# Cosine attention and a hard-swish MLP on one core: the written-out order of pairs 0 to 17 is replaced by another

## The chip, the cores and the metric

The kernel runs on one NeuronCore of one Trainium2 chip. The core has five engines that run their own instruction queues in order and wait for one another through semaphores: TensorE (PE; its weight loads are listed as PEld), VectorE (DVE), ScalarE (ACT), GpSimd (POOL) and SyncE (SP), which here only issues DMAs. The metric is the device time of one launch in microseconds (us). The kernel before takes 404.92 us, the median of three runs (403.64, 404.92 and 406.51).

## The reference: what is computed

```python
q_n = q / (np.linalg.norm(q, axis=-1, keepdims=True) + 1e-06)
k_n = k / (np.linalg.norm(k, axis=-1, keepdims=True) + 1e-06)
scores = np.matmul(q_n, k_n.transpose(0, 1, 3, 2)) / tau
attn = softmax(scores)                       # over the last axis
x = np.matmul(attn, v)                       # then heads side by side: (3584, 768)
h = x @ w_in                                 # (3584, 2048)
g = h * np.clip(h + 3.0, 0.0, 6.0) / 6.0
out = g @ w_out                              # (3584, 768), float32
```

q, k and v have 8 batches, 12 heads, 448 rows and 64 columns. The excerpt is shortened: the softmax of the reference is written out with its maximum and its sum.

## The kernel before, in words

**Tiling.** Two heads make a pair, so there are 8 x 6 = 48 pairs, and six pairs make a batch. Loads, squares and norms work on items: item j is q or k for two pairs, 128 partitions by 896 float32 (448 KB). For the first items the two pairs' halves (448 columns each) can also be handled apart. For a pair the kernel squares, sums over the head dimension, takes the norm, scales the rows, transposes them on TensorE, copies the transposes out of PSUM, multiplies K by Q (scores), takes the exponential on ScalarE, multiplies by V (values), divides by the sum, and transposes the result back into `xT`, the MLP's input. When the six pairs of a batch are in `xT`, the MLP of that batch can run: 16 units of six matmuls with `w_in` (each followed by a relu on ScalarE and a product on VectorE), and later the products with `w_out`.

**What sets the order.** Pairs 18 to 47 are written by a loop that repeats. Pairs 0 to 17 are written out as a list, `PLAN` (line 21), of tokens, which `run` (line 973) turns into instructions one after another. Each engine executes its own instructions in exactly that order. An instruction waits only for what it reads and for the buffer that it writes, so a token far down the list can start at once when its engine is free, and a token whose input is late holds up everything behind it on its engine. The loads (`LQ`, `LV`) are issued by SyncE in list order too.

**The tokens.** The number behind the name is the item j or the pair i. A letter `a`, `v` or `p` names the engine: ScalarE, VectorE or GpSimd.

- `LQ.j` loads item j (line 197), `LV.d` loads V for two pairs with four DMAs (line 212), `W` issues one load of weights from GpSimd's queue (line 923).
- `SQ.j.e.c.n` squares n column groups of item j from group c on engine e (lines 227 and 229). `RE.j` sums the squares on VectorE (line 241); a further number means one half.
- `NO.d` makes 1/norm of items 2d and 2d+1: four small ScalarE operations (lines 269, 270, 275, 276), or with `v` two on ScalarE and two on VectorE (lines 272, 273).
- `NM.j.e` multiplies item j by 1/norm (line 286); a further number means one half. On VectorE, this and `SQ` read two operands from SBUF.
- `TR.j` transposes item j on TensorE (line 332). `CQ.i`, `CK.i`, `CS.i` copy Q and K of pair i out of PSUM (line 354 on VectorE, 352 on ScalarE).
- `SC.i.g` is group g of the scores (lines 432 and 435), `EX.i.g` its exponential (line 453); up to pair 5 the exponential of groups 0 to 2 is one instruction of 128x896, from pair 6 on it is two of 128x448.
- `VC.i.e` casts V of pair i (line 305; on VectorE line 303), `VA.i.g` multiplies by V (line 475), `FI.i` divides by the sums (lines 495, 496).
- `BK.i` transposes back (line 509), `CX.i` copies into `xT` (line 354 or 352); later pairs use DMA transposes (`XD`, `XB`, `XP`).
- `U` is the next matmul unit of the MLP (line 580 for `w_in`, line 627 for `w_out`), `UA` and `UV` its work on ScalarE and VectorE (lines 589 and 595). The 36 units of the plan belong to batches 0 and 1.
- `WS` and `GL` are sums and copies of weights and of `gT` on VectorE.
- `DP.n` and `D.n` are n matmuls on zeros, whose results nobody reads (lines 935 and 930). `OPEN` (`open_ring`) frees the PSUM of the first six pairs and makes six banks, which scores, transposes and units use in turn from then on.

The two banks (`SC`) of the first six pairs are used in turn: scores of a group wait until the exponential of the group before last has read its bank.

Of the kernel before, what the change touches and what calls it, by code (L numbers as in the profile page):

```python
# [1110 lines left out]
```

## Time and profile before

The profiled execution's span, from its first to its last instruction, is 404.4 us; the median of the three unprofiled runs is 404.92 us.

| engine | busy, us | share of the span | instructions |
|---|---|---|---|
| TensorE matmul | 393.7 | 97% | 3689 |
| TensorE weight load | 234.5 | 58% | 3689 |
| VectorE | 288.7 | 71% | 512 |
| ScalarE | 276.7 | 68% | 604 |
| GpSimd | 236.7 | 59% | 232 |

The granted TensorE clock is 1.000 over the span. The 16 DMA engines move 63.75 MB. Matmuls are pipelined: a group of six matmuls with `w_in` takes 1.14 us in the chain of work although one of them is listed with 352 ns, so a busy TensorE in these rows is not yet one that works at its full rate.

How to read the rows that follow: a row of the timeline gives the start and the length in us, the engine, the line of the kernel, the operation, what it writes and reads with shapes, how many instructions are merged in the row, and in brackets how long the engine had been idle and what released it. A row of stretches gives the busy time of each engine within the stretch. A row of a group gives the count, the busy time and the mean length in ns.

### The profile page before, as it was taken

The numbers are of one execution on the slowest core, as the hardware profiler recorded it, in microseconds if no ns is written. First come the engines' busy times: TensorE is split into PE (matmuls) and PEld (weight loads), VectorE is DVE, ScalarE is ACT, GpSimd is POOL, SyncE is SP. The second block draws the span as 40 slices with busy tenths as digits, with TensorE's granted clock in tenths as the row PEclk, the third lists the DMA queues.
The fourth block names the chain that finished last, engine by engine and source line by source line (L and its number), as shares of the span: only waits on it lengthen the run. The fifth ranks groups of instructions, "written<-read, shape, count | busy, mean of one in ns | idle before, by whom it ended". The sixth has DMA issues, their size and how long they took to land.

```text
span 404.4 us, 9618 instructions
## 1 busy us (share of the span) xinstructions
PE 393.7 (97%) x3689; PEld 234.5 (58%) x3689; DVE 288.7 (71%) x512; ACT 276.7 (68%) x604; POOL 236.7 (59%) x232
## 2 busy tenths in 40 slices
PE   7798999999999999999999999999999999999996
PEld 5566656555665555655555556555565556555564
DVE  5898787878498777777857887587656666655663
ACT  4899989887377687687768768768758755225230
POOL 4799945862744997588486875876664600510070
PEclk9999999999999999999999999999999999999999
DMA  8899999999877748786779659986863523140134
GB/s 285 247 235 243 221 221 213 170 219 202 181 168 179 167 111 209 185 222 129 169 200 194 140 149 163 180 190 136 193 147 76 112 45 63 36 88 20 25 74 99
DMA packets 93166, 63.75 MB, mean 158 GB/s; under 512 B 56128, under 2 KB 93120, under 8 KB 93120
## 3 DMA queue, kind: packets, MB, share of 16 engines
q1 hardware_dynamic: 87408, 56.45, 61.1%
q0 software_dynamic: 5312, 6.29, 9.5%
q8 instruction: 29, 0.48, 0.6%
q10 hardware_dynamic: 400, 0.39, 0.3%
q14 instruction: 17, 0.14, 0.1%
HBM read 45.61 MB, written 11.01 MB: 140 GB/s over the span
## 4 chain that ended last, share of the span: by engine, by line
PE 88%; ACT 4%; DVE 3%; DMA 3%; SPq 1%; issue 0%; DVEq 0%; ACTq 0%
PE M L580 23%; PE M L753 16%; PE PV L475 11%; PE Y L580 6%; PE Z L580 6%; PE M L435 6%; PE Z L753 5%; PE Y L753 4%; PE M L833 3%; PE M L627 3%; ACT at L453 3%; DMA big<-in_q_dram 3%; PE Y L435 1%; PE Z L435 1%; PE Y L833 1%; PE Y L627 1%
## 5 line engine op out<-in xcount | busy, mean ns | idle before, releaser
L453 ACT ACTIVATE at<-M 128x448 bf16<-128x448 f32 x194 | 96.8, 564 | 23.2 <-PE M L435 20.7
L580 PEld LDWEIGHTS <-w_in_sb 128*128 128x128 bf16 x768 | 72.3, 98 | 63.1 <-issue 2.5
L580 PE MATMUL M<-xT,w_in_sb 128*128 128x448 bf16 x504 | 107.4, 352 | 0.1
L286 POOL TENSOR_TENSOR nrm<-big,r 128x896 bf16<-128x896 f32 (+1 forms) x47 | 78.1, 1665 | 14.8 <-issue 4.6
L229 POOL TENSOR_TENSOR big<-big 128x896 f32<-128x896 f32 (+5 forms) x45 | 68.1, 1519 | 14.8 <-DMA big<-in_k_dram 8.2
L589 ACT ACTIVATE u<-M,bias 128x448 bf16<-128x448 f32 x84 | 54.9, 655 | 26.3 <-PE M L580 26.0
L475 PEld LDWEIGHTS <-at 128*128 128x128 bf16 (+1 forms) x1536 | 54.1, 97 | 19.9 <-issue 12.1
L595 DVE SCALAR_TENSOR_TENSOR gT<-u,M 128x448 bf16<-128x448 bf16 x73 | 44.6, 617 | 29.2 <-ACT u L589 28.4
L475 PE MATMUL PV<-vx,at 128*128 128x65 bf16 (+1 forms) x1536 | 62.7, 194 | 0.0
L241 DVE TENSOR_REDUCE n<-big 128x14 f32<-128x896 f32 (+1 forms) x50 | 51.5, 1037 | 0.3 <-ACT big L227 0.2
L392 POOL COPY km<-tT 64x128 bf16<-64x128 bf16 x34 | 14.4, 424 | 61.9 <-PE M L435 25.9
L782 POOL TENSOR_TENSOR big<-big 128x384 f32<-128x384 f32 x11 | 11.8, 1077 | 54.6 <-ACT big L801 54.5
L753 PEld LDWEIGHTS <-gT 128*128 128x128 bf16 x288 | 27.8, 98 | 20.0 <-DVE gT L731 0.6
L753 PE MATMUL M<-w_out_sb,gT 128*128 128x384 bf16 x192 | 35.0, 326 | 0.1
L496 DVE TENSOR_TENSOR on<-PV,rc 128x512 bf16<-128x512 f32 x48 | 33.2, 691 | 1.7
L435 PE MATMUL M<-tT,kz 64*128 64x448 bf16 (+1 forms) x171 | 30.9, 351 | 0.5 <-ACT at L453 0.5
L453 ACT ACTIVATE at<-Y 128x448 bf16<-128x448 f32 x50 | 28.2, 564 | 4.3 <-PE Z L435 4.3
L753 PEld LDWEIGHTS <-gs 128*128 128x128 bf16 x224 | 21.5, 98 | 14.7 <-DVE gs L731 0.3
L453 ACT ACTIVATE at<-Z 128x448 bf16<-128x448 f32 x50 | 28.2, 565 | 2.6 <-PE M L435 2.6
L305 POOL CAST vx<-big 128x512 bf16<-128x512 f32 x39 | 28.2, 728 | 3.1 <-DMA big<-in_v_dram 3.0
L580 PE MATMUL Z<-xT,w_in_sb 128*128 128x448 bf16 x132 | 28.6, 353 | 0.0
L580 PE MATMUL Y<-xT,w_in_sb 128*128 128x448 bf16 x132 | 28.6, 352 | 0.0
(128 smaller groups left out, 574.7 us busy)
## 6 DMA issues: line engine op xcount, KB each, us to landing
big<-in_k_dram SPq DMA_DIRECT2D x24, 448.0 KB, 5.1
big<-in_q_dram SPq DMA_DIRECT2D x24, 448.0 KB, 4.5
out_dram<-o SPq DMA_DIRECT2D x107, 96.0 KB, 2.2
big<-in_v_dram SPq DMA_DIRECT2D x48, 128.0 KB, 4.7
big<-in_v_dram SPq DMA_DIRECT2D x48, 96.0 KB, 4.4
w_in_sb<-in_moe_w_in_dram POOLq DMA_DIRECT2D x8, 384.0 KB, 10.4
w_out_sb<-in_moe_w_out_dram POOLq DMA_DIRECT2D x4, 768.0 KB, 10.8
tT<-nrm SPq DMA_TRANSPOSE x34, 2.8
```

What stands on the lines that cost most here:

```text
L229: engines[e].tensor_tensor(out=o, in0=i, in1=i, op=ALU.mult)
L241: nc.vector.tensor_reduce(out=n2_and_r[0][:, d % 2, j % 2, c], in_=sq[:, :, :, :].rearrange("p g c d -> p (g c) d")[:, c, :], axis=AX.X, o ...
L286: engines[e].tensor_tensor(out=nrm[:, :, g, :].rearrange("p c g d -> p g c d"), in0=raw_of[j][:, g, :, :], in1=n2_and_r[4][:, d % 2, j % 2, :]
L305: (engines[e].copy if e == "a" else engines[e].tensor_copy)(out=o, in_=f)
L435: nc.tensor.matmul(o, ks, qt[rows], start=True, stop=True)
L453: nc.scalar.activation(out=o, in_=x, func=AF.Exp, scale=inv_tau)
L475: nc.tensor.matmul(pv_out(j, h), at[rows, n, q_cols(i // HP, j)], vt[rows, 3 + h if name == "M" else 5 * h + int(name[1]), :], start=(name ...
L496: nc.vector.tensor_tensor(out=on[:, :, :, :].rearrange("p j h d -> p h j d"), in0=pv4[:, :, :, 0:D], in1=rc[:, :, :].to_broadcast([128, 2, ...
L580: nc.tensor.matmul(ps[:, 0:S], w_in_sb[:, cc, fc * 128 : (fc + 1) * 128], x[:, cc, 0:S], start=(cc == 0), stop=(cc == CC - 1),)
L589: nc.scalar.activation(out=u[:, :], in_=ps[:, 0:S], func=AF.Relu, bias=half_bias, scale=1.0 / 6.0)
L595: nc.vector.scalar_tensor_tensor(out=g[:, fc, c0 : c0 + S], in0=u[:, :], scalar=1.0, in1=ps[:, 0:S], op0=ALU.min, op1=ALU.mult,)
L753: nc.tensor.matmul(m, lhs[:, c, :], rhs[:, c, c0 : c0 + width], start=(base is None and c == 0), stop=(c == KC - 1), skip_group_check=True,)
```

## The change: another list for pairs 0 to 17

All lines of `PLAN` are replaced; no function, no tile and nothing from pair 18 on is changed. The new list holds the same attention and MLP work. These things differ:

- The order. Item 0 is loaded before item 1. 41 matmuls on zeros stand together ahead of the first transpose; in all there are 90 of 248 columns, where the list before had 87, and two of 512 columns that are gone.
- The engine of some operations. Of the squares, counted in items of 896 columns, GpSimd has 9.9 instead of 14.8, ScalarE 8.8 instead of 5.6, VectorE 4.3 instead of 2.6. Of the scaling (`NM`), GpSimd has 15.5 items instead of 17.5 and VectorE 5.5 instead of 3.5. Of the casts of V, GpSimd keeps 11, ScalarE has 7 instead of 2 and VectorE 2 instead of 7. Four norms instead of two use VectorE for their second half. Of the copies into `xT`, VectorE has 9 instead of 7 and ScalarE 1 instead of 3; ScalarE has two copies of Q instead of one.

The diff, cut to the part up to the first unit (`U`) and a few later lines:

```diff
--- before.py
+++ after.py
 PLAN = [
-    "DP.1 LQ.1 DP.2 DP.1 DP.1 DP.1 DP.1 DP.1 SQ.1.a.0.4 SQ.1.a.7.4 DP.1 SQ.1.v.4.3 DP.1 SQ.1.p.11.3 LQ.0 DP.2 DP.3",
-    "LQ.3 DP.1 LQ.2 SQ.0.p.6.2 RE.1.0 RE.1.1 LQ.5 DP.2 SQ.0.a.0.6 SQ.0.p.8.6 DP.1 RE.0.0 RE.0.1 DP.1 NO.0.1 DP.1 DP.1",
-    "NM.1.v.1 DP.1 SQ.3.a.0.7 DP.1 LQ.4 DP.2 D.2 DP.1 DP.2 NM.1.v.0 LV.0 DP.1 DP.2 NO.0.0.v DP.4 SQ.2.a.0.7 TR.1.Y",
-    "CK.1.a DP.1 DP.1 DP.1 DP.2 RE.3 DP.1 RE.2 NM.0.p.1 CK.0.a SQ.5.a.4.3 DP.2 DP.1 DP.4 DP.1 LQ.8 NM.0.p.0",
-    "SQ.4.v.4.3 SQ.5.a.0.4 NO.1 DP.1 DP.2 SQ.4.p.0.4 LV.1 TR.0.Z DP.3 DP.1 DP.1 NM.3.p LQ.7 NM.2.p.0 CQ.0.v SC.0.0.0",
-    "RE.5 LQ.6 DP.1 DP.1 EX.0.0 SC.0.1.1 DP.1 RE.4 NM.2.v.1 EX.0.1 DP.1 DP.1 NO.2 NM.4.p DP.1 LQ.10 VC.0.v DP.1 DP.2",
-    "LQ.9 DP.1 SC.0.2.0 SC.0.3.1 TR.3.Y CQ.1.v VC.1.v LV.2 CK.2.v DP.2 DP.2 DP.1 DP.1 VC.2.v EX.0.2 SQ.7.p.0.7 LQ.11",
-    "W EX.0.3 TR.2.Z CQ.2.v SC.1.0.0 EX.1.0 SC.1.1.1 CQ.3.v DP.1 SC.1.2.0 TR.4.Z VC.3.v EX.1.1 EX.1.2 SC.1.3.1 VA.0.0",
-    "CQ.4.v EX.1.3 DP.1 CQ.5.v LV.4 DP.2 LV.3 SQ.6.a.0.7 NM.5.v.1 W DP.1 DP.1 RE.7 SC.2.0.0 RE.6 VA.0.1 NM.5.p.0",
-    "SC.2.1.1 VA.0.2 VA.0.3 SQ.8.p.0.7 EX.2.0 EX.2.1 DP.3 SQ.9.p.0.7 DP.1 SC.2.2.0 FI.0 CK.3.v TR.5.Z SC.2.3.1 EX.2.2",
-    "CK.4.v NO.3.v NM.6.p RE.8 VA.1.0 VA.1.1 SC.3.0.0 VA.1.2 VA.1.3 EX.2.3 SC.3.1.1 FI.1 EX.3.0 SC.3.2.0 EX.3.1",
-    "EX.3.2 SC.3.3.1 EX.3.3 VA.2.0 SQ.10.p.0.7 RE.9 SQ.11.p.0.7 W NM.7.p.0 VC.4.p CK.5.v DP.1 VA.2.1 VA.2.2 VA.2.3",
-    "FI.2 VC.5.p LQ.13 NO.4 SC.4.0.0 TR.6.Y SC.4.1.1 EX.4.0 CQ.6.v CQ.7.v VA.3.0 VA.3.1 RE.10 VA.3.2 NM.8.p SC.4.2.0",
-    "BK.2.Z EX.4.1 EX.4.2 VC.6.p VA.3.3 NM.9.p W W VC.7.p LQ.12 LV.5 SC.4.3.1 SC.5.0.0 CX.2.v NM.7.v.1 FI.3 EX.4.3",
-    "BK.0.Y CX.0.v SC.5.1.1 EX.5.0 EX.5.1 SC.5.2.0 BK.3.Y DP.1 RE.11 TR.7.Z CX.3.v VA.4.0 VA.4.1 SQ.13.p.0.7 CK.6.v",
-    "SC.5.3.1 EX.5.2 BK.1.Y NO.5 NM.10.p EX.5.3 OPEN VA.4.2 CK.7.v SQ.12.p.0.7 SC.6.0 DP.1 CS.7.v VA.4.3 EX.6.0",
-    "CX.1.v CS.6.v SC.6.1 SC.6.2 TR.8 SC.6.3 EX.6.1 W W LQ.15 FI.4 VA.5.0 BK.4.Y VA.5.1 VA.5.2 CQ.8.v CQ.9.v EX.6.2",
-    "VC.8.p CX.4.v SC.7.0 VA.5.3 VC.9.p FI.5 TR.9 SC.7.1 EX.6.3 EX.7.0 SC.7.2 SC.7.3 CK.8.v CS.9.v CK.9.v VA.6.0",
-    "VA.6.1 CS.8.v VA.6.2 VA.6.3 BK.5 CX.5.v EX.7.1 SC.8.0 LQ.17 EX.7.2 EX.7.3 U EX.8.0 NM.11.p SC.8.1 SC.8.2 FI.6",
...
-    "UA CX.8.v U VA.12.3 SC.13.0 UV SC.13.1 UA FI.12 UV EX.13.0 U XD.14 VC.13.a SQ.19.a.0.4 SQ.19.p.4.3 GL.0 SC.13.2",
-    "SQ.18.v.0.7 U EX.13.1 VA.13.0 SC.13.3 CS.14.v XD.15 U VA.13.1 UA RE.19 LQ.21 UA UV U CK.14.a UV W EX.13.2",
...
-    "U FI.16 CK.18.v UA U WS.y4.0 SC.17.3 EX.17.3 CS.18.v CK.19.v UV XB.16 VA.17.0 NM.20.v",
+    "LQ.0 SQ.0.a.8.6 SQ.0.p.6.2 RE.0.1 SQ.0.a.0.6 RE.0.0 LQ.1 SQ.1.a.0.4 SQ.1.a.11.3 SQ.1.p.4.3 RE.1.0 LQ.2 LQ.3",
+    "SQ.1.p.7.4 RE.1.1 NO.0.0 NM.0.v.0 NO.0.1 NM.1.v.1 SQ.2.a.0.7 NM.1.v.0 NM.0.p.1 DP.4 DP.4 DP.4 DP.4 DP.4 DP.4",
+    "DP.4 DP.4 DP.4 DP.4 DP.1 TR.0.Z CQ.1.v CQ.0.a DP.2 TR.1.Y CK.0.v DP.4 DP.1 SC.0.0.0 RE.2 SQ.3.a.0.7 RE.3",
+    "SC.0.1.1 CK.1.v LQ.4 LQ.5 EX.0.0 EX.0.1 LV.0 SQ.5.v.0.4 LQ.7 W NO.1.v DP.4 DP.4 SC.0.2.0 DP.3 SC.0.3.1 LQ.6",
+    "SQ.5.v.4.3 EX.0.2 EX.0.3 DP.4 DP.2 SC.1.0.0 DP.1 SC.1.1.1 EX.1.0 NM.2.v.1 DP.4 SC.1.2.0 NM.2.v.0 LV.1 LQ.8",
+    "SQ.4.a.4.3 EX.1.1 TR.2.Z RE.5 SQ.4.p.0.4 RE.4 EX.1.2 NM.3.p DP.3 SC.1.3.1 EX.1.3 TR.3.Y VC.0.p LQ.9 VA.0.0",
+    "VA.0.1 CQ.2.v CK.2.v VA.0.2 VC.1.p VA.0.3 CK.3.v NO.2.v FI.0 SQ.7.a.0.7 RE.7 SC.2.0.0 LV.2 CQ.3.v NM.4.p VC.2.p",
+    "SC.2.1.1 EX.2.0 DP.4 DP.3 SC.2.2.0 SQ.6.a.0.7 NM.5.p.0 RE.6 VA.1.0 VA.1.1 VA.1.2 VA.1.3 FI.1 TR.4.Z CQ.5.v",
+    "CQ.4.v EX.2.1 SC.2.3.1 EX.2.2 EX.2.3 VC.3.p LV.4 BK.0.Y LV.3 LQ.11 CX.0.v DP.1 SC.3.0.0 DP.1 SC.3.1.1 NO.3.v",
+    "NM.5.p.1 W VA.2.0 W VA.2.1 VA.2.2 VA.2.3 EX.3.0 EX.3.1 NM.7.p.0 SC.3.2.0 EX.3.2 LQ.10 NM.6.p NM.7.p.1 SQ.8.p.0.7",
+    "SQ.9.v.0.7 BK.1.Y LQ.13 TR.5.Z CK.4.v SC.3.3.1 EX.3.3 DP.2 SC.4.0.0 DP.1 SC.4.1.1 FI.2 DP.1 VA.3.0 EX.4.0 EX.4.1",
+    "VA.3.1 VA.3.2 VA.3.3 CX.1.v CK.5.v LQ.14 RE.9 BK.2.Z SC.4.2.0 SC.4.3.1 CX.2.v TR.6.Y FI.3 VC.4.a CQ.6.v TR.7.Z",
+    "VC.5.p EX.4.2 SC.5.0.0 LQ.12 EX.4.3 CQ.7.v CK.6.v VA.4.0 CS.6.v SC.5.1.1 VA.4.1 VA.4.2 VA.4.3 W EX.5.0 SC.5.2.0",
+    "RE.8 BK.3.Y EX.5.1 EX.5.2 W FI.4 CX.3.v SC.5.3.1 CS.7.v NO.4 EX.5.3 OPEN CK.7.v DP.3 SC.6.0 BK.4.Y VA.5.0 VA.5.1",
+    "VA.5.2 CX.4.v DP.1 VA.5.3 EX.6.0 SC.6.1 SC.6.2 EX.6.1 NM.8.v FI.5 VC.6.p TR.8 CQ.8.v SC.6.3 W VA.6.0 VA.6.1",
+    "EX.6.2 EX.6.3 CQ.9.v BK.5 SC.7.0 CX.5.v EX.7.0 NM.9.v SQ.11.p.0.7 RE.11 VA.6.2 SC.7.1 SC.7.2 VA.6.3 FI.6 EX.7.1",
+    "EX.7.2 U SQ.10.p.0.7 VC.8.p TR.9 VC.7.a CK.8.a SC.7.3 CS.9.v EX.7.3 RE.10 CK.9.v U VA.7.0 VA.7.1 VA.7.2",
+    "SQ.13.p.0.7 UA UA VC.9.p CS.8.v UV U NO.5 SC.8.0 SC.8.1 UV UA EX.8.0 NM.11.p UV EX.8.1 U UA UV VA.7.3 FI.7",
...
+    "RE.16 LQ.21 EX.13.3 U SQ.18.a.0.7 U UV UV GL.0 VC.14.a CK.15.v LQ.20 FI.12 VA.13.0 UA SQ.19.p.0.4 UA UA U U U",
+    "VA.13.1 VA.13.2 RE.19 RE.18 SQ.21.a.0.7 SQ.20.a.0.7 UV UV UA VC.15.p UA UV UV UA NN.8 U UV UV UA UV SC.14.0",
+    "EX.14.0 W W SC.14.1 EX.14.1 LV.9 LV.8 U UA VA.13.3 FI.13 UV U U UA UA CS.14.v SC.14.2 NM.16.p EX.14.2 SC.14.3",
+    "XD.16 NM.19.p RE.20 VC.16.a U VA.14.0 VA.14.1 NM.17.v XD.17 RE.21 XP.12 UV UV EX.14.3 UA SC.15.0 SC.15.1 SC.15.2",
+    "EX.15.0 SQ.22.v.4.3 EX.15.1 EX.15.2 VA.14.2 VA.14.3 FI.14 VC.18.a LQ.23 U SC.15.3 CK.17.a CK.16.v NM.18.p",
+    "EX.15.3 CS.16.v WS.6 XD.18 U UA UV NO.10.v VA.15.0 VA.15.1 SC.16.0 SC.16.1 EX.16.0 SC.16.2 WS.7.1 EX.16.1",
+    "VA.15.2 VC.17.a VA.15.3 FI.15 XP.14 WS.7.0 XD.19 U UV SC.16.3 VA.16.0 VC.19.a CK.18.v VA.16.1 EX.16.2 WS.1 LV.11",
...
+    "SC.17.3 CK.19.a UV CS.18.v VA.17.0 SQ.22.v.0.4 XB.16 EX.17.3",
 ]
```

27 rows, old and new, of the table PLAN are left out of this document.

## The prediction

> **What bounds the kernel now.** I read the page first, then the stretches of the span, then the timeline of the opening, then ScalarE's groups.
>
> ```profile
> span 404.4 us, 9618 instructions
> PE 393.7 (97%) x3689; PEld 234.5 (58%) x3689; DVE 288.7 (71%) x512; ACT 276.7 (68%) x604; POOL 236.7 (59%) x232
> ```
> ```profile
> 4.28:14.90 10.62, 9.02 (x70) 6.84 (x68) 7.47 (x14) 7.02 (x20) 4.96 (x6) 1.00 0.95 299
> 14.90:44.00 29.10, 26.71 (x396) 17.96 (x396) 26.27 (x62) 27.97 (x53) 28.53 (x25) 1.00 1.12 247
> 44.00:117.00 73.00, 72.90 (x715) 42.21 (x715) 55.45 (x100) 56.66 (x126) 41.17 (x38) 1.00 1.01 199
> 117.00:341.00 224.00, 223.87 (x2155) 131.69 (x2152) 163.24 (x265) 165.67 (x373) 145.62 (x136) 1.00 0.69 154
> ```
> The stretches give, after the length, the busy us of PE, PEld, DVE, ACT and POOL. The last one quoted is the loop of pairs 18 and up: PE is busy 223.87 of 224.00 us, so what happens there can't be hastened by an order of pairs 0 to 17; it can only begin earlier or later. The same is nearly true from 44 us on. Between 14.90 and 44.00 it is another matter: ACT (27.97), POOL (28.53) and DVE (26.27 of 29.10) are all nearly full, and PE fills its time with attention and zeros. So the kernel's time is a fixed amount of PE work behind the first MLP unit, plus the time at which that unit can start. The question is when it starts after the change, and whether PE stays fed from there to pair 18.
>
> ```profile
> 2.47 5.55 PE L935 MATMUL PV<-xT 128*128 128x248 bf16 x26 [2.47 <-DVE vx L988]
> 4.28 0.72 ACT L227 ACTIVATE big<-big 128x256 f32<-128x256 f32 x2 [2.26 <-DMA big<-in_k_dram]
> 5.49 0.52 ACT L227 ACTIVATE big<-big 128x384 f32<-128x384 f32 x1 [0.49 <-DMA big<-in_q_dram]
> 6.11 1.26 DVE L241 TENSOR_REDUCE n<-big 128x7 f32<-128x448 f32 x2 [0.22 <-ACT big L227]
> 7.29 1.15 DVE L286 TENSOR_TENSOR nrm<-big,r 128x448 bf16<-128x448 f32 x2
> 8.40 1.22 PE L935 MATMUL PV<-xT 128*128 128x248 bf16 x10
> 9.46 0.55 PE L332 MATMUL Y<-ident,nrm 128*128 128x128 bf16 x7
> 9.81 0.94 ACT L227 ACTIVATE big<-big 128x896 f32<-128x896 f32 x1
> 10.47 1.83 POOL L286 TENSOR_TENSOR nrm<-big,r 128x448 bf16<-128x448 f32 x2 [3.75 <-DVE r L273]
> 12.36 0.56 PE L332 MATMUL Z<-ident,nrm 128*128 128x128 bf16 x7 [0.55 <-POOL nrm L286]
> 13.59 0.56 DVE L229 TENSOR_TENSOR big<-big 128x384 f32<-128x384 f32 x1 [1.27 <-DMA big<-in_q_dram]
> 14.06 0.38 DVE L354 COPY tT<-Z 128x448 bf16<-128x448 bf16 x1
> 14.50 0.36 PE L435 MATMUL SC<-tT,kz 64*128 64x448 bf16 x2 [1.05 <-DVE tT L354]
> 14.90 1.73 ACT L453 ACTIVATE at<-SC 128x896 bf16<-128x896 f32 x2 [0.99 <-PE SC L435]
> ```
> The reader is to see a late first score. K of pairs 0 and 1 is transposed at 9.46, but Q is scaled on POOL only at 10.47, behind a norm whose end waits for other work, and transposed at 12.36. Its copy out of PSUM then stands on DVE behind a square whose load comes at 13.59. So scores start at 14.50 and exponentials at 14.90.
>
> **The change part by part.**
>
> *The opening.* Item 0 takes item 1's place in the queue of loads, so its squares start at 4.28 and item 1's at 5.49. DVE still makes four half reduces and ends them at about 7.3, as now (6.11 + 1.26). The first norm runs beside them, so the first half `NM` on DVE starts at about 7.3. The second norm's four ACT operations take about 1.1 us to 8.4; two more halves on DVE at 1.15 for two end at 9.6, and one half goes to POOL. 41 zeros stand ahead of the first transpose: 26 took 5.55 us, the other 15 go at 0.11 each (1.22 for 10), so they end at 2.47 + 5.4 + 1.6 = 9.5 and cover this wait. Item 0 is transposed at 9.5, item 1 at about 10.0 (0.55 each), its copy on DVE ends at about 11.0, and the first score starts at 11.1: 3.4 us before 14.50. Nothing of this waits for the fifth or the sixth load. ACT meanwhile does one copy and the square of item 3 (whose load is there by 9.81), so the first exponential starts at about 11.5, again 3.4 earlier.
>
> *From the first exponential to the first unit.* Here ACT is full, and I count what it does besides exponentials.
>
> ```profile
> L227 ACT ACTIVATE big<-big 128x896 f32<-128x896 f32 x3 | 2.9, 955 | 1.6 <-DMA big<-in_k_dram 1.6
> L275 ACT ACTIVATE le<-nr,bias 128x28 f32<-128x28 f32 x7 | 2.2, 319 | 0.2
> L269 ACT ACTIVATE ln<-n 128x28 f32<-128x28 f32 x8 | 1.9, 232 | 0.0
> L270 ACT ACTIVATE nr<-ln 128x28 f32<-128x28 f32 x8 | 1.8, 227 | 0.3
> L276 ACT ACTIVATE r<-le 128x28 f32<-128x28 f32 x7 | 1.6, 227 | 0.6
> L305 ACT CAST vx<-big 128x512 bf16<-128x512 f32 x2 | 1.3, 640 | 0.0
> L352 ACT COPY xT<-M 128x448 bf16<-128x448 bf16 x2 | 1.0, 556 | 0.0
> L352 ACT COPY kz<-Y 128x384 bf16<-128x384 bf16 x1 | 0.5, 479 | 0.5 <-DVE kz L354 0.5
> ```
> A whole norm is 232 + 227 + 319 + 227 = 1.0 us, one that ends on DVE 0.46. Before, between the first exponential and the end of pair 7's: three whole norms, one half norm, one square: 3.0 + 0.46 + 0.95 = 4.4 us. After: one whole norm, three half norms, two squares of 896, one of 384 (0.52), one cast: 1.0 + 1.4 + 1.9 + 0.5 + 0.6 = 5.4. So ACT, 3.4 us early at the start, is 2.4 us early at the end of pair 7.
>
> ```profile
> 41.69 1.42 ACT L453 ACTIVATE at<-M 128x448 bf16<-128x448 f32 x3
> 43.40 0.58 ACT L453 ACTIVATE at<-Z 128x448 bf16<-128x448 f32 x1
> 43.29 0.38 PE L509 MATMUL M<-ident,on 128*128 128x128 bf16 x4 [0.16 <-DVE kz L354]
> 43.71 0.39 DVE L354 COPY xT<-M 128x448 bf16<-128x448 bf16 x1 [0.47 <-PE M L509]
> 43.90 1.31 PE L580 MATMUL M<-xT,w_in_sb 128*128 128x448 bf16 x6
> ```
> In front of the first unit (43.90) stands the last copy into `xT` (43.71), and before it the transposes that wait for DVE's copies of K. In the new list that copy stands ahead of pair 9's work on DVE, and the unit needs only pair 7's first exponential, which ends some 2.4 us before its last (41.6 against 43.98). By ACT the unit could start at 43.98 - 2.4 - 2.4 = 39.2, by DVE, whose list from the first score to that copy is about as long as it was (three squares and two ends of norms more, four casts of V and four copies fewer) and took 43.9 - 14.5 = 29.4 us, at 11.1 + 29.4 = 40.5. I take 40.0. PE has done less by then: scores of two groups (0.36 and 0.29) and one transpose (0.39 at its rate) are behind the unit instead of before it, 0.9 us. The zeros are as many (90 for 87, and two of 512 columns fewer) and all still ahead of the unit. Gain at this point: 43.9 - 40.0 - 0.9 = 3.0 us.
>
> *From the first unit to pair 18.* ACT gets more here: four casts more (2.6), three squares for 0.63 of one (2.2), one copy of K more (0.5), pair 7's last exponential (0.6), a half norm more (0.5), two copies into `xT` fewer (-1.1): +5.2 on 56.66 of 73.00 us. On average that fits, but not in its first part.
>
> ```profile
> 44.00:50.00 6.00, 6.00 (x65) 3.46 (x65) 4.19 (x9) 5.27 (x11) 6.00 (x8) 1.00 1.20 213
> 50.00:55.00 5.00, 4.90 (x35) 2.31 (x32) 4.01 (x7) 4.30 (x12) 4.99 (x4) 1.00 1.18 214
> ```
> ACT has 0.73 + 0.70 = 1.4 us of idle time in the first 11 us behind the unit, and of the added work about 2.7 us (a cast, a copy, a norm moved here, the exponential) falls there. The overhang, 1.3 us, is what I charge to PE; later additions meet a freer ACT and cost nothing, unless loads are late. POOL's load is taken up below.
>
> *VectorE and GpSimd on SBUF.* How they hinder each other is in the trace:
>
> ```profile
> 15.01 4.61 POOL L286 TENSOR_TENSOR nrm<-big,r 128x896 bf16<-128x896 f32 x3
> 16.35 0.82 DVE L286 TENSOR_TENSOR nrm<-big,r 128x448 bf16<-128x448 f32 x1
> L286 POOL TENSOR_TENSOR nrm<-big,r x47: 935/1687/2402, 10.5 to 312.5; 128x896 bf16<-128x896 f32 x42, 128x448 bf16<-128x448 f32 x5
> L286 DVE TENSOR_TENSOR nrm<-big,r x6: 614/636/1080, 7.3 to 117.3; 128x448 bf16<-128x448 f32 x5, 128x896 bf16<-128x896 f32 x1
> ```
> At 16.35 a half `NM` on DVE took 0.82 instead of 0.61 beside POOL's, so 0.2 was lost. Below zero I can bound this: DVE can't win back more than such losses, 0.2 here. Above: each two-operand operation of DVE may wait for a whole one of POOL, 1.69. Behind the opening and before the unit the new list has seven of these on DVE (four before). POOL itself has 8.1 squares and scalings of 896 columns fewer before the unit, 8.1 x 1.69 = 13.7 us of the 33.5 that it works between 4.28 and 44, so it is no bound any more, and meetings are rarer. I take nothing, the value nearest to the row of 16.35, and keep the upper end for a rival. The Trainium skill ("SBUF — State Buffer", section "Who interferes with whom") says that a DVE instruction with two SBUF inputs and a GpSimd instruction that reads SBUF exclude each other, and that whichever issues first blocks the other for its whole length; the row of 16.35 agrees with that.
>
> **Sum:** -3.0 + 1.3 = -1.7 us. On the span of 404.4 that is 402.7; the median of the runs is 0.5 above the span, and on it the forecast is 404.92 - 1.7 = 403.2.
>
> **Rivals.**
>
> *The lead arrives whole.* The unit starts at 39.2 as ACT allows, the overhang hides behind banks already filled: -3.8 + 0 = 401.1, with the runs' spread 400.4 to 401.8. For it: six PSUM banks lie between PE and ACT from the unit on. Against it: DVE, as full as ACT there. Chance 0.20.
>
> *ScalarE takes PE's place.* PE waits not for 1.3 but for some 3.0 of the 5.2 us added, since units, scores and exponentials share the banks and one late evacuation holds PE: 404.9, no change. For it: ACT's 5.27 of 6.00. Against it: 16 us of idle ACT time in the stretch as a whole. Chance 0.22.
>
> *Slower: VectorE is shut out.* By the rule above, if POOL always has an operation in hand when DVE comes, a wait of up to 1.69 is added in front of copies that PE needs. One such wait whole takes the gain away (1.7); from two on the kernel is slower; four of the seven cost 6.8, so 404.9 - 1.7 + 6.8 = 410.0. For it: `NM.2`, `SQ.9` and `NM.9` on DVE stand beside POOL's `NM.3`, `NM.7` and `SQ.11`. Against it: the one such meeting above cost 0.2. Chance 0.13. That the new list leaves meetings as they are, so that the change doesn't do what it says, would alter only this term.
>
> **How the numbers follow.** My forecast, 403.2 (402 to 404.4), has 0.45. The range 400.3 to 407.5 takes it in with the first two rivals and the cheaper half of the third; it leaves out its dear half and the rim of the first, under 2 in 10. About 1% (4.0 us) is what a measurement of this kernel can tell from no change. Faster than 400.9 is the lower half of the first rival: 0.10. Slower than 409.0 is most of the third: 0.12. Within: 0.78.
>
> **What would show it.** First score at 11.1 and first exponential at 11.5 on the timeline; the first unit at about 40.0; ACT above 95% busy from 11.5 to 50; PE's idle time and stretched rows between 40 and 55; the scores of pair 18 about 1.7 us before their present place, and the same length from there to the end. I am wrong if the first score is late (a load, or POOL's half of item 0), if `NM` or `SQ` rows on DVE of over 1.3 us are frequent before 45 us, or if PE waits after 60 us for squares whose load came late.

## The result and the profile after

The changed kernel takes 410.47 us (median of four runs, 408.23 to 412.12) against 405.05 (403.64 to 406.51) for the kernel before on the same chip: 1.0138 times as long, 95% interval 1.0093 to 1.0183. Measured a second time (e13_changed_again below) it was 410.75 against 404.28, 1.0141 (1.0117 to 1.0165). It is slower by 1.4%; 403.2 was forecast. The profiled execution has a span of 406.2 us and took 408.23, the shortest of the four; about 2 us lie around every span.

First the page of the changed kernel, then its stretches, cut at its own first exponential (11.3), first unit (43.4) and first exponential of pair 18 (119.5).

```profile
span 406.2 us, 9634 instructions
PE 393.1 (97%) x3690; PEld 233.7 (58%) x3690; DVE 293.1 (72%) x517; ACT 281.4 (69%) x606; POOL 225.3 (55%) x225
```
```profile
11.30:43.40 32.10, 26.96 (x397) 17.73 (x397) 28.10 (x60) 27.06 (x49) 23.37 (x23) 1.00 0.95 235
43.40:119.50 76.10, 75.06 (x737) 44.08 (x734) 61.63 (x112) 63.77 (x140) 36.64 (x34) 1.00 0.90 194
119.50:343.50 224.00, 224.00 (x2149) 131.73 (x2147) 162.34 (x266) 165.54 (x372) 145.18 (x135) 1.00 0.68 155
```

The same cuts of the kernel before, profiled once more (the run e8_before_again below; first exponential 12.4, first unit 42.6, pair 18 at 116.3):

```profile
12.40:42.60 30.20, 26.78 (x395) 18.00 (x394) 27.45 (x62) 28.09 (x53) 28.42 (x25) 1.00 1.06 257
42.60:116.30 73.70, 73.60 (x723) 42.69 (x722) 56.50 (x101) 57.33 (x129) 41.79 (x40) 1.00 0.97 195
116.30:340.30 224.00, 224.00 (x2151) 131.99 (x2148) 160.24 (x266) 165.09 (x372) 144.84 (x135) 1.00 0.68 154
```

From pair 18 on the two kernels take nearly the same time, as forecast: 286.7 us to the end after the change (406.2 - 119.5), 286.4 before (402.7 - 116.3). The opening is 1.1 us shorter (11.3 against 12.4), the stretch up to the first unit 1.9 longer, and the one from there to pair 18 2.4 longer: +3.2 together, against +3.5 of span. In the first of these stretches no engine is full after the change: ACT is busy 27.06 of 32.10 us (84%), where it had 28.09 of 30.20, and POOL 23.37 where it had 28.42. GpSimd and ScalarE did get free time; the work between them got slower all the same.

The timeline of the changed kernel shows the opening, the first place where it stalls, one scaling further on (`NM.8`) and the first unit:

```profile
10.75 0.55 PE L434 MATMUL SC<-tT,kz 64*128 64x448 bf16 x4
11.26 1.72 ACT L452 ACTIVATE at<-SC 128x896 bf16<-128x896 f32 x2
...
14.26 1.72 POOL L285 TENSOR_TENSOR nrm<-big,r 128x896 bf16<-128x896 f32 x1 [1.45 <-DVE r L272]
14.36 3.05 DVE L285 TENSOR_TENSOR nrm<-big,r 128x448 bf16<-128x448 f32 x2
15.93 1.96 POOL L304 CAST vx<-big 128x512 bf16<-128x512 f32 x2
17.47 0.56 PE L331 MATMUL Z<-ident,nrm 128*128 128x128 bf16 x7 [1.52 <-DVE nrm L285]
18.70 0.55 ACT L452 ACTIVATE at<-SC 128x448 bf16<-128x448 f32 x1 [1.14 <-PE SC L431]
...
39.16 1.15 DVE L285 TENSOR_TENSOR nrm<-big,r 128x896 bf16<-128x896 f32 x1
...
43.41 1.29 PE L579 MATMUL Z<-xT,w_in_sb 128*128 128x448 bf16 x6
```

The two halves of `NM.2` on DVE take 3.05 us instead of 1.2 (2 x 0.614, the shortest of this group): POOL's `NM.3` started 0.1 us ahead of them, and POOL's two casts run beside the second. TensorE idles 1.52 us for them, and ScalarE 1.14 for the scores behind. The kernel before, in its second profile, opens like this:

```profile
11.10 0.56 DVE L229 TENSOR_TENSOR big<-big 128x384 f32<-128x384 f32 x1 [0.23 <-DMA big<-in_q_dram]
...
12.01 0.36 PE L435 MATMUL SC<-tT,kz 64*128 64x448 bf16 x2
12.41 0.92 ACT L453 ACTIVATE at<-SC 128x896 bf16<-128x896 f32 x1 [0.24 <-PE SC L435]
...
42.62 1.31 PE L580 MATMUL M<-xT,w_in_sb 128*128 128x448 bf16 x6
```

The square on DVE that started at 13.59 in the prediction's rows starts at 11.10 here: the sixth load landed at 11.0 us, not at 13.5. So the first profile of the kernel before (span 404.4, about 406.4 us with what lies around it) was of a late load, and the second (span 402.7, 404.51 us) is the one near the median.

The largest waits of TensorE and ScalarE between 12 and 43.4 us (sum, times, longest), first in the changed kernel, then before:

```profile
PE PV L934 <- DVE on L495: 2.3, 3, 1.0
ACT at L452 <- PE SC L431: 1.7, 2, 1.1
PE Z L331 <- DVE nrm L285: 1.5, 1, 1.5
PE M L434 <- ACT at L452: 1.2, 1, 1.2
ACT at L452 <- PE SC L434: 1.1, 3, 0.8
```
```profile
PE SC L435 <- ACT at L453: 1.2, 4, 0.4
PE Z L332 <- POOL nrm L286: 0.8, 1, 0.8
ACT at L453 <- PE SC L435: 0.7, 2, 0.4
PE SC L432 <- ACT at L453: 0.5, 1, 0.5
PE M L435 <- ACT at L453: 0.5, 1, 0.5
```

Before, TensorE mostly waits for ScalarE's exponentials: ScalarE sets the pace. After, TensorE waits for VectorE, and ScalarE for TensorE. The first row is of zeros: line 934 writes the bank that VectorE's division (`FI`) reads, so a zero waits for it, and the scores queued behind the zero wait too.

### The profile page after: what moved, and what is told of

Same layout as the page of the kernel before. It is cut to its first block, busy times and chain, and to the rows that moved or that the text cites. A ratio compares the mean times of both kernels' runs of the same rounds, so it can differ in the third digit from the quotient of the medians.

```text
span 406.2 us, 9634 instructions
## 1 busy us (share of the span) xinstructions
PE 393.1 (97%) x3690; PEld 233.7 (58%) x3690; DVE 293.1 (72%) x517; ACT 281.4 (69%) x606; POOL 225.3 (55%) x225
## 4 chain that ended last, share of the span: by engine, by line
PE 85%; ACT 5%; DMA 3%; DVE 2%; SPq 2%; POOL 1%; issue 1%; DVEq 0%; ACTq 0%; POOLq 0%
PE M L579 22%; PE M L752 16%; PE PV L474 10%; PE Z L579 6%; PE Y L579 6%; PE Z L752 5%; PE M L434 5%; PE Y L752 4%; PE M L832 3%; ACT at L452 3%; PE M L626 3%; DMA big<-in_v_dram 2%; SPq L211 2%; PE Y L434 1%; PE Z L434 1%; DMA big<-in_k_dram 1%
## 5 line engine op out<-in xcount | busy, mean ns | idle before, releaser
L285 POOL TENSOR_TENSOR nrm<-big,r 128x896 bf16<-128x896 f32 (+1 forms) x45 | 75.2, 1675 | 27.8 <-ACT r L275 12.6
L228 POOL TENSOR_TENSOR big<-big 128x896 f32<-128x896 f32 (+5 forms) x40 | 59.9, 1500 | 19.5 <-DVE n L240 15.5
L452 ACT ACTIVATE at<-Z 128x448 bf16<-128x448 f32 x50 | 28.5, 569 | 1.8 <-PE M L434 1.7
```

The costliest lines, as they stand in the source:

```text
L228: engines[e].tensor_tensor(out=o, in0=i, in1=i, op=ALU.mult)
L285: engines[e].tensor_tensor(out=nrm[:, :, g, :].rearrange("p c g d -> p g c d"), in0=raw_of[j][:, g, :, :], in1=n2_and_r[4][:, d % 2, j % 2, :]
L452: nc.scalar.activation(out=o, in_=x, func=AF.Exp, scale=inv_tau)
```

## Experiments

Times are medians; a ratio is to runs of the kernel before on the same chip, and a gain or loss beside it is worked out from the ratio. Tokens are those of the list.

### What the kernel before does

The kernel before without an edit:

> The kernel before, unchanged, for a second profile. In the first one the sixth load landed at 13.5 us and VectorE's square of item 4, which stands ahead of the first copy of Q, waited for it, so the first score came at 14.5. In the changed kernel's profile the sixth load landed at 11.0. If that difference belongs to the execution and not to the order, an execution of the kernel before of 403.5 to 404.5 us shows the sixth load at about 11 and the first exponential at 12.5 to 13.5, and most of the 3.6 us by which the changed order starts its exponentials earlier isn't there to be won. If the early landing belongs to the changed order, this profile again shows about 13.5 and 14.9.

404.51 us, span 402.7, first exponential 12.4, as shown above. The 3.4 us of the forecast's opening were measured from a late load; from this run they are 1.1.

```diff
- SQ.4.v.4.3 ... CQ.0.v
+ CQ.0.v SQ.4.v.4.3
```

> The kernel before, but VectorE's square of item 4, which waits for the sixth load, stands behind the first copy of Q instead of ahead of it. If the late load sets the start in its slower runs (405.8 to 407.1) and not in its faster ones (403.5 to 404.6), the slower ones disappear or come down by about 1 us and the median falls by 0.3 to 1 us. If the first score isn't what the end hangs on, because GpSimd and ScalarE are full behind it, the median stays within 0.3 us of 404.4 and the spread stays.

404.83, ratio 1.0004 (0.9985 to 1.0023). The square that waits for the sixth load, in front of the copy of Q, costs the kernel before nothing that can be told in the median.

### Single suspects before the first unit

```diff
- NM.2.v.1 ... NM.2.v.0
+ NM.2.p
```

> The changed kernel, but the scaling of item 2 is one operation on GpSimd, ahead of item 3's, instead of two halves on VectorE beside it. In the changed kernel's profile those halves take 2.1 and 1.0 us instead of 0.6 each, because GpSimd's scaling of item 3 and a cast of V run at the same time. If this meeting is what loses the early lead, the transposes of item 2 come at about 16.1 instead of 17.5 us, pair 2's first exponential at about 19 instead of 20.7, and the kernel is 1.5 to 2 us faster than the changed one (about 408.7). If the meeting is covered by something later (late loads, ScalarE), the time stays within 0.7 us of 410.5.

409.58, ratio 1.0113 (1.0080 to 1.0145). The meeting is gone: `EX.1.3` starts at 17.3 instead of 18.7. But pair 2's exponential starts at 20.61, against 20.7, because POOL now does `NM.2` and `NM.3` one behind the other, as the timeline of this run shows:

```profile
16.84 1.68 POOL L285 TENSOR_TENSOR nrm<-big,r 128x896 bf16<-128x896 f32 x1
18.58 0.56 PE L331 MATMUL Y<-ident,nrm 128*128 128x128 bf16 x7 [1.46 <-POOL nrm L285]
20.61 0.92 ACT L452 ACTIVATE at<-SC 128x896 bf16<-128x896 f32 x1 [1.25 <-PE SC L434]
```

The wait of 1.5 us has only changed its owner. The gain is about 1 us, and the intervals overlap. In this trace another operation is stretched instead: `NM.9`, 2.47 us on VectorE beside a square on GpSimd, where it took 1.08 in the changed kernel's trace.

```diff
- SQ.5.v.0.4 LQ.7 ... SQ.5.v.4.3 ... NM.2.v.0
+ LQ.7 ... NM.2.v.0 SQ.5.v.0.7
```

> The changed kernel, but VectorE's square of item 5 (the sixth load) is one operation behind its scaling of item 2, not ahead of the end of norm 1. If the changed kernel loses because VectorE stands still for the sixth load in those runs where loads come late (it landed at 11.0 us in the changed kernel's profile, at 13.5 in that of the kernel before), this takes 2 to 3 us off the median (about 408) and narrows the spread of its runs. If the wait for the load is not the cause, the time stays within 0.7 us of 410.5, and the meeting of item 2's scaling with GpSimd's stays as it is.

410.12, ratio 1.0127 (1.0092 to 1.0162): no gain that can be told, so the square of a late load ahead of `NM.2` isn't the cause.

```diff
+ SC.1.3.1 ahead of TR.2; EX.2.1 SC.2.3.1 ahead of TR.4; EX.4.0 SC.4.2.0 ahead of VA.3.0
```

> The changed kernel with three groups of scores moved ahead in TensorE's queue: SC.1.3 ahead of item 2's transposes, SC.2.3 ahead of item 4's, SC.4.2 ahead of pair 3's values (with the exponentials that they wait for moved ahead too). In the changed kernel's profile ScalarE stands idle for 1.1, 0.6 and 0.8 us at exactly these places, while the scores wait behind work that waits for VectorE. If TensorE's order there loses the lead, pair 5's last exponential ends 1.5 to 2.5 us earlier (36 instead of 38.1) and the kernel takes about 408. If VectorE's chain (norms, copies, divisions) is what sets the pace, ScalarE is only idle elsewhere and the time stays within 0.7 us of 410.5.

409.81, ratio 1.0120 (1.0089 to 1.0151). Little or nothing: pair 5's last exponential ends at 37.8 us, where 36 was hoped for and 38.1 is the changed kernel's, so these scores' place in TensorE's queue is not what holds ScalarE up.

### Halves of the two lists put together

The kernel before up to `OPEN` (just behind pair 5's last exponential), then what the changed list has left:

> The order of the kernel before up to where pair 5's last exponential has been put in the queue, and the changed order from there (what the first part has done already left out). If the loss arises in the first 38 us, this is about as fast as the kernel before, 405 to 406. If ScalarE's added casts and squares behind the first unit are what costs, it is about 2 to 3 us slower than the kernel before (407 to 408), with the stretch from 44 us to pair 18 about 2 us longer.

407.05, ratio 1.0052 (1.0022 to 1.0081): 2.1 us slower than before (0.9 to 3.3). That is what the changed order behind pair 5 costs in this composition. In its trace the stretch from the first unit to pair 18 is 75.5 us, 1.9 longer than before, which agrees with the 2.4 us by which it has grown in the changed kernel. The seam has a wait of its own, 1.5 us in front of pair 6's first score (0.5 before), so the figure is not the order's alone.

The other way round:

> The changed order up to where pair 5's last exponential has been put in the queue, and the order of the kernel before from there. If the loss arises in the first 38 us (meetings on SBUF, late loads), this is 3 to 5 us slower than the kernel before (408 to 410). If ScalarE's added work behind the first unit is the cause, the early first score is kept and this is 0 to 2 us faster than the kernel before (403 to 405).

413.80, ratio 1.0216 (1.0182 to 1.0250). The seam itself made a hole, so this run doesn't price the first half:

```profile
44.09 0.23 ACT L268 ACTIVATE ln<-n 128x28 f32<-128x28 f32 x1 [4.92 <-DVE n L240]
44.50 0.53 PE L434 MATMUL Z<-tT,kz 64*128 64x448 bf16 x1 [4.41 <-DVE kz L353]
```

Only the opening (up to `EX.0.1`) from the changed list, the rest from the one before:

> The changed list up to its second exponential, then the list before. If the opening of the new list is worth the lead that the two traces show where both have their loads at 11 us (first exponential 11.3 against 12.4), and the order behind it is what loses time, then 404.6 - 1.1 = 403.5 us, first unit at about 41.5. If a lead of the opening is lost in any case, because ScalarE and GpSimd are nearly full until the first unit, then 404.6 and the first unit at 42.6 as before.

407.65, ratio 1.0086 (1.0054 to 1.0118): 3.5 us slower, not 1.1 faster. The first exponential starts at 11.5, but the third at 17.3, later than in the second profile of the kernel before (15.1) and in the changed kernel (13.3). Item 5 is now the sixth load (landed at 11.2; as the fifth it landed at 9.3), and the exponentials brought forward push its square on ScalarE back further, to 13.1 from 10.1. VectorE's sum of it follows, and the next norms stand behind that:

```profile
14.14 2.08 DVE L240 TENSOR_REDUCE n<-big 128x14 f32<-128x896 f32 x2 [0.50 <-ACT big L226]
16.26 0.23 ACT L268 ACTIVATE ln<-n 128x28 f32<-128x28 f32 x1 [1.16 <-DVE n L240]
16.97 0.56 PE L331 MATMUL Y<-ident,nrm 128*128 128x128 bf16 x7 [2.43 <-POOL nrm L285]
```

So an early first exponential isn't a lead by itself here; the squares and norms of the next pairs must come forward with it.

### Behind the first unit

The kernel of e3_front_before with eight operations moved from ScalarE to GpSimd:

```diff
- VC.14.a VC.16.a VC.17.a VC.18.a VC.19.a SQ.18.a.0.7 SQ.20.a.0.7 SQ.21.a.0.7
+ VC.14.p VC.16.p VC.17.p VC.18.p VC.19.p SQ.18.p.0.7 SQ.20.p.0.7 SQ.21.p.0.7
```

> The same kernel as the one with the front of the kernel before and the changed order behind it (407.05 us), but five casts of V (pairs 14 and 16 to 19) and three squares (items 18, 20, 21) that the changed order gives to ScalarE are on GpSimd, 5 us of ScalarE's time. If ScalarE's added work is what the part behind the first unit loses, the time falls to about 405.3, and ScalarE's busy time between 44 and 117 us from some 62 to 57 us. If the order of that part loses it by itself, the time stays within 0.7 us of 407.05.

413.65, ratio 1.0234 (1.0193 to 1.0275). GpSimd also issues the loads of weights (`W`), and two of these were issued at 89.9 us, behind the added work, instead of 83.7 in e3_front_before:

```profile
101.44 1.44 PE L627 MATMUL M<-w_out_sb,gT 128*128 128x384 bf16 x4 [3.73 <-DMA w_out_sb<-in_moe_w_out_dram]
```

So GpSimd has no room for these eight operations in this list. What they cost on ScalarE this run can't show, because the late weights cover it.

```diff
- VC.7.a CK.8.a
+ VC.7.p CK.8.v
```

> The changed kernel with one cast of V (pair 7) on GpSimd and one copy of K (pair 8) on VectorE instead of ScalarE, both in the first 11 us behind the first unit: 1.1 us less on ScalarE there. If ScalarE's overhang is what TensorE waits for behind the unit, 409.9 - 1.1 = 408.8 us, with fewer TensorE waits between 45 and 62 us. If those waits are set by VectorE's copies or by the order, 409.9 or a little more (VectorE gets 0.4).

408.98, ratio 1.0111 (1.0088 to 1.0134). The interval overlaps with that of the changed kernel, and in the trace the stretch from the first unit to pair 18 is 75.9 us instead of 76.1. These two operations of ScalarE are not what TensorE waits for there: its waits that are left (0.5, 0.2 and 0.2 us) are all for VectorE.

### The zeros

The changed kernel without its 17 zeros between the first exponential of pair 2 and the first unit:

```diff
- EX.2.0 DP.4 DP.3 SC.2.2.0 ... DP.1 SC.3.0.0 DP.1 SC.3.1.1 ... DP.2 SC.4.0.0 DP.1 SC.4.1.1 FI.2 DP.1 ... DP.3 SC.6.0 ... DP.1 VA.5.3
+ EX.2.0 SC.2.2.0 ... SC.3.0.0 SC.3.1.1 ... SC.4.0.0 SC.4.1.1 FI.2 ... SC.6.0 ... VA.5.3
```

> The changed kernel without the 17 zero matmuls between the first exponential of pair 2 and the first unit. They write the bank from which VectorE divides, and in the trace three groups of them wait 0.96, 0.73 and 0.59 us for that, with scores queued behind. If the zeros hold the scores: 1 to 2.3 us less, 407.6 to 408.9, and the first unit at 41 to 42.4. If the scores behind them would wait anyway (for their bank or for a copy of K): 409.9, unchanged; if TensorE's clock needs them, the clock falls and the time is longer.

407.56, ratio 1.0067 (1.0046 to 1.0089), apart from the changed kernel's 1.0117 to 1.0165: 3.0 us won (0.0074 of 404.3), the largest gain of any single edit of the changed kernel and more than the zeros' own 1.9 us (17 x 0.11). The trace doesn't show where it comes in: it is of the longest of the six runs (408.81, mean clock 0.992), and its first unit is at 44.2, not between 41 and 42.4 as expected.

The same zeros, each placed behind the first product with V of the next pair:

```diff
+ VA.1.0 DP.4 DP.3 ... VA.2.0 DP.2 ... VA.3.0 DP.4 ... VA.5.0 DP.3 ... VA.6.0 DP.1
```

> The changed kernel with the same 17 zeros, each moved from ahead of the scores to behind the first product with V of the next pair, which waits for the same division anyway. If the loss was the wait of the zeros with scores queued behind it, as much is won as by leaving the zeros out, 2 to 2.5 us (407.8), and the clock keeps its full value more often, which may add up to 1.5. If leaving the zeros out helped only by their TensorE time (17 x 0.11 = 1.9 us), nothing is won here: 410.

409.25, ratio 1.0137 (1.0100 to 1.0174): no gain that can be told, where leaving them out gave one. Whether it is their place or their presence that costs is not settled by this, for its runs lie wide apart (408.09 to 413.18). In the traces of both runs a wait of 2.2 us for an exponential appears behind pair 5 (1.16 in the changed kernel), and behind it TensorE's clock is at half for some 3.4 us.

The kernel before without its 7 zeros in that stretch:

```diff
- DP.3 SQ.9.p.0.7 DP.1 SC.2.2.0 ... DP.1 VA.2.1 ... DP.1 RE.11 ... DP.1 CS.7.v
+ SQ.9.p.0.7 SC.2.2.0 ... VA.2.1 ... RE.11 ... CS.7.v
```

> The kernel before without its 7 zeros between the first exponential of pair 2 and the first unit. There no zero waits for VectorE, and TensorE waits for exponentials (0.2 to 0.5 us, six times). If ScalarE sets the pace of that stretch in the kernel before, 404.5, no change; if the zeros hold scores there too, 403.7, which would beat both kernels.

404.95, ratio 1.0012 (0.9992 to 1.0031). In the kernel before, where TensorE waits for ScalarE's exponentials, these zeros cost nothing that can be told.

### Several at once

First the edits of e1_nm2_pool, e5_scores_first, e10_unit_less_act and e11_no_late_zeros in one kernel; then those of e1_nm2_pool, e10_unit_less_act and e14_zeros_behind.

> The changed kernel with four repairs at once: NM.2 on GpSimd, the three scores moved ahead, the two ScalarE operations moved away behind the unit, and no late zeros. If the front loses its time in separate waits, the gains add: 0.9 + 0.5 + 1.1 + 1.5 = 4, so about 406. If one wait only takes the place of another, because no engine has work in hand when it is released, then 408 to 409.

408.30, ratio 1.0093 (1.0074 to 1.0112): no more was won than by e11_no_late_zeros alone (the intervals overlap).

> The same with NM.2 whole on GpSimd and the two operations behind the first unit taken from ScalarE. If the three losses are separate, 410 - 2.3 - 0.9 - 1.0 = 405.8, still not below before. If they share waits, 407 to 408.

409.04, ratio 1.0108 (1.0087 to 1.0129). The gains don't add: in both traces the wait behind pair 5 is 2.2 us instead of 1.16, with the clock at half behind it.

### TensorE's clock

The changed kernel again:

> The changed kernel itself once more, as the measure for the three runs beside it: 410 us, 1.013 times before.

410.75, ratio 1.0141 (1.0117 to 1.0165). Its five runs are 408.51 us at a mean clock of 0.999, 410.09 at 0.996, and 410.75, 410.86 and 410.92 at 0.994. The trace is of one with 0.994 (span 408.9). Its stretches of 1 us, TensorE's row (busy, then the granted clock behind POOL):

```profile
16.00:17.00 1.00, 0.38 (x3) 0.11 (x2) 1.00 (x1) 1.00 (x2) 1.00 (x2) 1.00 1.15 275
17.00:18.00 1.00, 0.00 (x0) 0.00 (x0) 1.00 (x2) 0.99 (x2) 1.00 (x2) 1.00 1.05 244
18.00:19.00 1.00, 0.81 (x8) 0.82 (x9) 1.00 (x2) 0.00 (x0) 0.60 (x1) 0.52 1.03 312
19.00:20.00 1.00, 1.00 (x7) 0.34 (x4) 1.00 (x2) 0.00 (x0) 0.00 (x0) 0.50 0.71 124
20.00:21.00 1.00, 1.00 (x11) 0.83 (x10) 0.41 (x2) 0.68 (x3) 0.00 (x0) 0.50 1.05 389
21.00:22.00 1.00, 1.00 (x29) 1.00 (x28) 0.82 (x4) 1.00 (x2) 0.00 (x0) 0.78 0.83 236
22.00:23.00 1.00, 0.78 (x14) 0.38 (x11) 0.92 (x3) 0.42 (x2) 0.57 (x1) 1.00 0.71 190
```

Behind the gap in front of `TR.2`, 1.81 us here and 1.52 in the first trace, the clock is at half for some 3.4 us. In the first trace it stayed at 1.00. The list is the same, and the first unit starts at 46.0 instead of 43.4. Of these 2.6 us, 0.7 are there already at `TR.2` (the sixth load landed at 13.5 here, at 11.0 in the first trace), 1.0 more at pair 5's last exponential, behind the stretch at half clock, and the last 0.9 come with `NM.8`, which took 2.03 us on VectorE instead of 1.15.

`NM.8` is a second meeting of VectorE and GpSimd on SBUF. Which of them comes first differs from run to run. The run e18_gap_no_late (below) shows it in full:

```profile
37.21 2.75 DVE L285 TENSOR_TENSOR nrm<-big,r 128x896 bf16<-128x896 f32 x1
37.31 1.69 POOL L228 TENSOR_TENSOR big<-big 128x896 f32<-128x896 f32 x1
...
40.02 0.56 PE L331 MATMUL M<-ident,nrm 128*128 128x128 bf16 x7 [1.58 <-DVE nrm L285]
```

VectorE's operation of 1.08 us ends only behind GpSimd's square, after 2.75, and TensorE waits 1.58 us with the transposes of item 8. In nine of the twelve traces of the changed kernel and of edits to it (lists put together from both kernels aside), the first unit starts 3.8 us plus the length of `NM.8` behind pair 6's first exponential; that length is 1.08 us in e10_unit_less_act, 1.15 in the first trace, 2.47 in e11_no_late_zeros. In the other three the clock was at half in that stretch. No run took `NM.8` off VectorE in the changed list, so what it costs in the median isn't measured.

Ten zeros more ahead of `TR.2`:

```diff
- EX.1.1 TR.2.Z
+ EX.1.1 DP.4 DP.4 DP.2 TR.2.Z
```

> The changed kernel with 10 zeros more ahead of the transpose of item 2 (TR.2), where TensorE is idle for 1.5 us in the first trace and 1.8 us, with the clock at half for 3.4 us behind it, in the second. If the halved clock costs what the runs of the changed kernel suggest (408.5 us at a clock of 0.999, 410.8 at 0.994), the mean clock comes back to 0.998 to 1.000 and the median to 408.5. If the clock falls only because the rest is slow, the median stays at 410.5.

411.67, ratio 1.0184 (1.0165 to 1.0202). In the trace the gap is filled (0.35 us left) and the clock there is 1.00, and pair 18 starts at 120.2, 1.9 earlier than in e13_changed_again (`NM.8` takes 1.91). But the median is no better, and the mean clock of the other runs is still 0.994 to 0.996. In the traced run time went at a place where the traces of the changed kernel and of e14_zeros_behind have no wait:

```profile
131.88 0.35 PE L579 MATMUL Z<-xT,w_in_sb 128*128 128x448 bf16 x1 [1.29 <-DMA xT<-on]
```

A unit of the next batch waits for the DMA transpose into `xT`. That this one gap makes the difference of 2 us is not borne out; a halved clock goes along with the longer runs, but that it is the cause isn't shown.

The same, and 13 late zeros left out:

> The same, and 13 of the 17 late zeros left out (the four behind OPEN stay, ahead of a wait of 1.2 us or more). If leaving out zeros gains by their own TensorE time and lost part of it to the clock (0.992 to 0.998 in those runs), 408.5 - 2.3 = 406.2. If the zeros filled waits, 408.5.

408.47, ratio 1.0090 (1.0068 to 1.0111): 3.2 us below e17_zeros_at_gap, so the gain from leaving zeros out is seen a second time. In the traces 1.9 us of it is there at pair 5's last exponential (36.1 against 38.0), `NM.8` takes 0.8 back (2.75 against 1.91), and 1.1 is left at pair 18 (119.1 against 120.2); the rest is at the wait for `xT`, 0.45 instead of 1.29 us, and what follows it. No kernel tried is faster than the one before.

## Why the prediction was wrong

**The bound.** Right: behind pair 18 little changed (0.3 us), and nearly all of the difference arises ahead of it.

**The opening, "3.4 us before 14.50/14.90".** The time forecast was right (first score 10.75 against 11.1, first exponential 11.26 against 11.5); the gain was wrong. The rows of before came from an execution whose sixth load was 2.5 us late, and that lateness is no property of the list. Against the second profile the gain is 1.1. This term was too large by 2.3 us, while the sum was put on a median that hardly contains the lateness: "0.5 above the span" set the median of other runs beside the span of this one, around which 2 us lie as around every other. The prediction's own row at 13.59, a DVE operation that waits for a load, was the warning.

**"Here ACT is full", the unit at 40.0.** This is the step that failed. It was 43.4. From the first exponential to the unit 28.5 us were forecast, 0.5 less than in the first profile of before (29.0); it took 32.1, 1.9 more than in the second (30.2). The step counted ScalarE's work and assumed that ScalarE would stay full; it was busy 84%, not over 95%. The bound by VectorE beside it took the old length over, 29.4 us from the first score to the unit, as if nothing in between would wait; it became 32.7 (10.75 to 43.41). The zeros were counted in total only (90 for 87); between the first exponential of pair 2 and the unit they are 17 instead of 7. The new order made TensorE wait for VectorE (1.5 us at `NM.2`, 2.3 in three groups of zeros) and ScalarE for TensorE, and neither was looked for in the new list. In the first trace the whole loss lies ahead of pair 5's last exponential (26.8 us from the first one, against 23.5 in the second profile of before); from there to the unit the new order took 1.4 less, so its idea of an earlier unit did work. Part of the cause is shown: leaving the late zeros out gave 3.0 us. The rest isn't settled: undoing the meeting at `NM.2` or moving scores gave about 1 us or less each, and together they didn't add.

**From the first unit to pair 18.** Right in size: a loss of 2.2 us (0.9 for work not done yet, 1.3 overhang) was forecast, 2.4 measured in the traces, 2.1 (0.9 to 3.3) in e3_front_before. The reason was not borne out: the cast and the copy taken from ScalarE changed the stretch by 0.2 us. The trace divides the loss otherwise: TensorE is busy 1.5 us longer in this stretch (75.06 against 73.60) and idle 0.9 longer, and its waits there (0.5, 0.4 and 0.2 us) are all for VectorE. ScalarE's own work grew by 6.4 us (63.77 against 57.33), not 5.2; the count had one added copy of K where the list has two. That later additions to ScalarE cost nothing agrees with the trace: from 73.0 us to pair 18 TensorE is busy 46.50 of 46.50 us.

**VectorE and GpSimd.** 0 was taken and a full wait each was the upper end. The 0 was wrong, and the reason "meetings are rarer" did not hold: GpSimd took up work from further down the list, so that it was busy 27.0 us between 4.28 and the unit, 6.5 less than the 33.5 before and not 13.7. The first meeting, `NM.2` beside `NM.3`, cost 1.9 us on DVE, so the rule that the prediction took from the Trainium skill ("SBUF — State Buffer", section "Who interferes with whom") agrees with the row at 14.36, and the 0.2 of the row at 16.35 was a poor guide. The second meeting is `NM.8`: 1.15 us in the first trace, but 2.03 in the second and between 1.08 and 2.79 in all of them. So the rival "VectorE is shut out" is right in kind, but its 410.0 is near by luck: it needed four such waits, and the traces show the first wherever `NM.2` is on VectorE and the second, over 1.3 us, in nine of twelve. The kernel before has one as well (half of `NM.5` took 1.89 us instead of 0.61 in its second profile). The operations that the rival named, `SQ.9` at 1.03 us and `NM.9` at 1.08, were not stretched in the first trace; and with the meeting at `NM.2` removed 409.6 remains.

**The sum.** Forecast -1.7; measured in spans, with the load on time in both, +3.5 (406.2 against 402.7). The 5.2 us between them are 2.3 of the opening, 2.4 of the stretch up to the unit (forecast 0.5 shorter, measured 1.9 longer), 0.2 behind the unit and 0.3 behind pair 18. The runs of the changed kernel lie another 2.2 us above its profiled one. In the one of them that was traced (e13_changed_again), 0.9 of it is `NM.8`. A lower mean clock goes with these runs; how much it costs, and why it falls in some, stays open.

## What to carry to other kernels

Profile the kernel before twice before subtracting its milestones: one load 2.5 us late in the only profile made a gain of 1.1 us look like 3.4. The same holds after the change: the first trace had `NM.8` at 1.15 us, and only the second showed that it meets GpSimd. When an order is changed, an engine that was full need not stay full: go through the new queue of TensorE and ask of each entry, zeros included, which other engine it now waits for. Taking load off an engine that isn't waited for bought nothing here, and adding to the one that queues the loads of weights made those late (a wait of 3.7 us).

## What was not expected of the hardware

- The first six loads of 448 KB end at 11.0 us in one trace of the kernel before and at 13.5 in another, for the same list.
- TensorE's clock fell to half behind a gap of 1.8 us, and stayed at 1.00 behind one of 1.5 us at the same place in another run of the same kernel. The length alone doesn't decide it: the clock fell behind a gap of 1.42 us in e11_no_late_zeros and stayed behind one of 1.58 in e18_gap_no_late. The Trainium skill ("TensorE: Matmul & The Clock Gate", section "Why this matters for your kernels") warns of gaps over about 3 us; here less was enough. The same page of the Trainium skill (section "What's actually happening") gives a window of about 3.4 us, which agrees with the 3.4 us at half clock.
- Of two halves of one operation on VectorE beside GpSimd, one took 2105 ns and the other 1025 instead of 614, and GpSimd's casts 0.98 each instead of 0.61: the two engines seem to have taken turns, one operation each. At `NM.8` in e18_gap_no_late the two lengths add up: 1.08 and 1.69 us alone, 2.75 measured.
